# One fixed instruction sequence behind the first block, and decayed k turned by VectorE and DRAM transfers

## The chip, the core and the metric

The kernel runs on one core of one Trainium2 chip. The core has five engines that work side by side, each through its own list of instructions in order: TensorE (PE, with weight loads shown apart as PEld), VectorE (DVE), ScalarE (ACT), GpSimd (POOL) and SyncE (SP), which issues most of the transfers. They wait for each other by semaphores. The metric is the device time of the program in microseconds; the median of three runs stands for a kernel.

## The reference

Two computations follow each other. The first is a linear recurrence over 768 steps, for 4 batches and 8 heads with 48 features; the second is a gated feed-forward block on the 3072 resulting rows.

```python
f = 1.0 / (1.0 + np.exp(-f_logit))
for t in range(S):
    state = f[:, :, t, :, None] * state + np.einsum('bhd,bhe->bhde', k[:, :, t], v[:, :, t])
    y[:, :, t] = np.einsum('bhd,bhde->bhe', q[:, :, t], state)
x = np.ascontiguousarray(y.transpose(0, 2, 1, 3)).reshape(B * S, H * D)      # 3072 x 384
g = x @ w_gate                                                             # 384 x 1536
silu = g * (1.0 / (1.0 + np.exp(-g)))
return (silu * (x @ w_val) @ w_out).astype(np.float32)                     # 1536 x 384
```

All of it is float32. The weights may come as 64-bit floats, in which case the kernel turns their bits into float32 itself.

## The kernel before, in words

The function `short_path` holds all the work that is timed; `general_path` runs behind it only if a flag says that some decay was too small for it.

**Attention.** The sequence is cut into six chunks of 128 steps. A unit is one batch and one chunk, so that there are 24. Inside a unit the recurrence is done by matmuls. Of the gates, running products are made from the back (`tail`, L527) and from the front (`head`, L552); k is multiplied by the first (`kT`, L550) and q by the second (`qT`, L553). Both lie with features on the partitions, two heads of 48 in one group of 128. The scores `sc` (L563) are eight matmuls with a contraction over 48 rows; VectorE masks them (`A`, L565). The output `y` adds 12 matmuls of the decayed state laid out in diagonal blocks with q (L587) and 16 matmuls of v with A (L596), each writing 32 partitions; ACT copies it into the token tile `xT` (L599). For the next state, the decayed k is needed with steps on the partitions: TensorE turns it in four transposes (`kt`, L570), ACT copies it out of PSUM (L572), and eight matmuls with v give `dS` (L603), which VectorE adds to the decayed state (L607). Chunk 5 needs no new state. From chunk 2 on (`SQUARES`), f, k and q are loaded in squares of 32 x 32 and turned by VectorE's own transposes (L519, L539, L540); before that TensorE turns them (L513).

**Feed-forward.** A block takes the 512 tokens of one chunk over all batches. Block 0 (`mlp_plain`) is done plainly: 12 gate and 12 value products of 512 columns (L655), while the weights are still being fetched and converted (`weight_piece`: ACT makes two parts, L455 and L457, VectorE joins them in four instructions, L463 to L467), and then the down product (L679). Blocks 1 to 5 (`mlp_fifteen`) use a bilinear scheme that makes 3 x 3 by 3 x 2 blocks with 15 products: VectorE first makes sums of tokens (`xs`, L717 to L723), and for each of four column tiles TensorE makes 15 products of two matmuls with 256 columns (L825), ACT copies the PSUM banks (L830) and VectorE combines them. A scheme with seven products follows for the down part (`down_seven`: twelve matmuls each, L923 and L977). The weights that these schemes use are sums too. They are made by VectorE in place: for half of the column tiles during block 0's down product (`weight_sums(0)`), for the other half and for the down weights during block 1.

**Order.** Block c runs beside the attention of chunk c + 1. `take_turns` emits a piece of the block, then a step of the attention, in turn. The instructions of the first chunk have a fixed order (`in_order`), and within a block some of the products are chained; otherwise a scheduler in the compiler decides, by its own reckoning of times, which instruction comes next on each engine. PSUM has eight banks: in blocks 1 to 5 two for A, one for B, two for o and c, three for attention.

Of the kernel before, what the change touches and what calls it, by code (L numbers as in the profile page):

```python
# [289 lines left out]
def short_path(ctx, tc, ident, least, judge, q, k, v, f_logit, moe_w_gate, moe_w_val, moe_w_out, out):  # L290
# [32 lines left out]
    early = ctx.enter_context(ExitStack())  # L323
    first_pool = early.enter_context(tc.tile_pool(name="first", bufs=1))
# [47 lines left out]
    decayed = const.tile([128, HP, D], FP32, tag="decayed", name="decayed")  # L372

    blocks = const.tile([128, HP, 2 * D], FP32, tag="blocks", name="blocks")
    nc.gpsimd.memset(blocks, 0.0)

    vs = [(const if i < NV // 2 else first_pool).tile([128, H, W], FP32, tag=f"v{i}", name=f"v{i}")
          for i in range(NV)]
    for t in vs:
        nc.gpsimd.memset(t[:, :, D:W], 0.0)  # L380

    w_both = const.tile([128, 2, KT, DFF], FP32, tag="w_both", name="w_both")
# [50 lines left out]
    def weight_piece(dst, src):  # L433
# [4 lines left out]

        if src.dtype == FP32:
            return (lambda: nc.sync.dma_start(out=dst, in_=src)), (lambda: None), (lambda: None)  # L440
        shape = list(dst.shape)
        kept = {}

        def fetch():
            kept["w"] = wst.tile(shape[:2] + [2 * shape[2]], I32, tag="w64", name="w64", bufs=3)
            nc.sync.dma_start(out=kept["w"], in_=src)

        def halves():
            words = kept["w"].rearrange("p a (n two) -> p a n two", two=2)
            return words[:, :, :, 0], words[:, :, :, 1]  # L450

        def sizes():
            lo, hi = halves()
            up = wst.tile(shape, I32, tag="up", name="up")
            nc.scalar.activation(up, lo.bitcast(U32), AF.Copy, scale=2.0 ** -29)  # L455
            top = wst.tile(shape, I32, tag="top", name="top")
            nc.scalar.activation(top.bitcast(FP32), hi.bitcast(FP32), AF.Abs)  # L457
            kept["up"], kept["top"] = up, top

        def join():  # L460
            lo, hi = halves()
            up, top = kept["up"], kept["top"]
# [3 lines left out]
            nc.vector.scalar_tensor_tensor(top, hi, -(1 << 30), top, op0=ALU.bitwise_and, op1=ALU.bitwise_or)  # L466
            nc.vector.tensor_tensor(dst.bitcast(I32), top, up, ALU.add)  # L467

        return fetch, sizes, join
# [10 lines left out]
    NW = 256  # L480

    def add_piece(dst, src):
        for group, f in zip((fetches, sizes, joins), weight_piece(dst, src)):
            group.append(f)

    for j in range(0, DFF, NW):
        for dst, src in ((w_gate, moe_w_gate), (w_val, moe_w_val)):
            add_piece(dst[:, :, j:j + NW], in_rows(src)[:, :, per * j:per * (j + NW)])
    for i in range(NF // 2):
        both = slice(i, NF, NF // 2)  # L490
        add_piece(w_out[:, both, :], in_rows(moe_w_out)[:, both, :])
# [12 lines left out]
    def attention(u):  # L504
# [12 lines left out]
        if c >= SQUARES:  # L517
            nc.scalar.activation(squares("f"), squares("f"), AF.Sigmoid)
            nc.vector.transpose(in_turn(pairs(gate)[:, :, 1:N1]), squares("f"))  # L519
# [3 lines left out]
        yield  # L523


# [8 lines left out]

        kT = att.tile([128, HP, C], FP32, tag="kT", name="kT")
        qT = att.tile([128, HP, C], FP32, tag="qT", name="qT")
        if c >= SQUARES:
            kp, qp = kT, qT
            nc.vector.transpose(in_turn(kT), squares("k"))  # L539
            nc.vector.transpose(in_turn(qT), squares("q"))  # L540
            load_after(u)
        else:
            kp = transposed("kTp", kr)
            qp = transposed("qTp", qr)
        if c:
            nc.vector.tensor_tensor(decayed, states[b], whole.broadcast_to((128, HP, D)), ALU.mult)
            for par in range(2):
                r = rows_of(par)
                nc.scalar.copy(blocks[r, :, par * D:(par + 1) * D], decayed[r])
        nc.vector.tensor_tensor(kT, kp, pairs(tail, 2)[:, :, 0:C], ALU.mult)  # L550
        head = att.tile([128, n], FP32, tag="head", name="head", bufs=1)
        nc.vector.tensor_tensor_scan(head, gate[:, 0:n], start, 1.0, op0=ALU.mult, op1=ALU.add)  # L552
        nc.vector.tensor_tensor(qT, qp, pairs(head)[:, :, 1:N1], ALU.mult)  # L553
        if 0 < c < SQUARES:
            load_after(u)
        yield
# [3 lines left out]
        for a in range(HP):  # L560
            for par in range(2):
                r = rows_of(par)
                nc.tensor.matmul(sc[par][:, a * C:(a + 1) * C], lhsT=kT[r, a, :], rhs=qT[r, a, :], start=True, stop=True)  # L563
        for par in range(2):
            nc.vector.tensor_tensor(A[:, par], sc[par].rearrange("p (a t) -> p a t", t=C),  # L565
                                    causal.unsqueeze(1).broadcast_to((128, HP, C)), ALU.mult)
        if c < NCH - 1:
            p = bank("kt")
            for a in range(HP):
                nc.tensor.transpose(p[:, a * C:(a + 1) * C], kT[:, a, :], ident)  # L570
            kt = att.tile([128, H, W], FP32, tag="kt", name="kt")
            nc.scalar.copy(kt, p.rearrange("t (h d) -> t h d", d=W))  # L572
        yield

        if b == 0:
            xT[c] = ffn.tile([128, KT, TB], FP32, tag="xT", name="xT", bufs=2)


        y = bank("y")

        def place(n):
            return y[Q * (n % 4):Q * (n % 4) + Q, n // 4 * C:(n // 4 + 1) * C]

        per = 2 * D // Q
        if c:
            for n in range(DM // Q):
                nc.tensor.matmul(place(n), lhsT=blocks[:, n // per, n % per * Q:(n % per + 1) * Q], rhs=qT[:, n // per, :],  # L587
                                 start=n < 4, stop=False, skip_group_check=True)
        flat = v_.rearrange("t h e -> t (h e)")
        met = {n % 4 for n in range(DM // Q)} if c else set()  # L590
        for par in range(2):
            for n in range(DM // Q):
                h = 2 * (n // per) + par
                at = n * Q - h * D
                if -Q < at < D:
                    nc.tensor.matmul(place(n), lhsT=flat[:, W * h + at:W * h + at + Q], rhs=A[:, par, n // per, :],  # L596
                                     start=n % 4 not in met, stop=par == 1 or at + Q <= D, skip_group_check=True)
                    met.add(n % 4)
        nc.scalar.copy(xT[c][:, :, b * C:(b + 1) * C], y[:, 0:DM].rearrange("p (a t) -> p a t", t=C))  # L599
        if c < NCH - 1:  # L600
            p = bank("dS")
            for h in range(H):
                nc.tensor.matmul(p[W * (h % 2):W * (h % 2) + W, (h // 2) * D:(h // 2 + 1) * D],  # L603
                                 lhsT=kt[:, h, :], rhs=v_[:, h, 0:D], start=True, stop=True)
            dS = p[:, 0:HP * D].rearrange("p (a d) -> p a d", d=D)
            if c:
                nc.vector.tensor_tensor(states[b], decayed, dS, ALU.add)  # L607
            else:
                nc.scalar.copy(states[b], dS)
        yield  # L610

    def load_after(u):

        w = u + (1 if units[u][1] >= SQUARES else 2)
        if w < len(units) and (units[w][1] >= SQUARES) == (w == u + 1):
            load(w)

    def attention_steps(c):

        runs = [attention(c * B + b) for b in range(B)]  # L620
        parts = [1, 2, 1, 1]
# [27 lines left out]
    def mlp_plain(c):  # L649
        h = {}  # L650

        def product(w, j, name):
            p = fps.tile([128, 512], FP32, tag="m", name=name)[:, 0:TB]
            for i in range(KT):
                nc.tensor.matmul(p, lhsT=w[:, i, j * 128:(j + 1) * 128], rhs=xT[c][:, i, :],  # L655
# [17 lines left out]
        return ([lambda j=j, f=f: f(j) for i in range(0, NF, 2) for f in (gate, val) for j in (i, i + 1)],  # L673
# [8 lines left out]
    def put_out(p, c, b):  # L682
        ob = ffn.tile([128, 2, DM], FP32, tag=f"ob{b % 2}", name="ob", bufs=1)[:, 0, :]
# [487 lines left out]
```

## Time and the profile before

| | |
|---|---|
| median of three runs | 632.69 us (630.79, 632.69 and 632.91) |
| the profiled execution, its whole time | 630.66 us |
| its span, first to last instruction | 628.9 us |
| VectorE busy | 497.9 us (79%) |
| ScalarE busy | 297.4 us (47%) |
| transfers on SP's queue | 84,144 packets, 42.68 MB, 28.6% of 16 DMA engines' time |
| first gate product of block 0 starts | 33.22 us |
| first product of block 1 starts | 146.88 us |
| last matmul ends | about 623.8 us |

A row of the profile names the line, the engine, the operation, what it writes and reads (`sc<-qT,kT`), its tile and a count. In rows of TensorE each float32 matmul has two records, so that `x16` is eight matmuls. A matmul's duration reaches into the next one's, since they are pipelined: how fast TensorE goes is read from start to start. In the table of stretches each row gives the stretch, its length, and the busy time of PE, PEld, DVE, ACT and POOL with the number of instructions; then the clock granted to TensorE and the share of the DMA engines' time.

### The profile page before, as it was taken

To read this page: it belongs to the slowest core of one execution; us is meant where nothing else is said; L and a number is where in the kernel's file an instruction comes from. 1 tells how busy PE (TensorE), PEld (TensorE's weight loads), DVE (VectorE), ACT (ScalarE), POOL (GpSimd) and SP (SyncE) were. 2 spreads that over 40 slices of the span, in tenths; PEclk is the share of its full clock that TensorE was granted. 3 is DMA by queue.
4 is the path that set the end of the run, shared out by engine and by line. 5 is a ranking of instruction groups with operands and counts; after the bars stand their busy time and mean duration, and the time that the engine had idled before them with its cause. 6 is when DMAs were issued, how large, how long until landed. Compare 5 with 4: busy or idle time off the path is not lost.

```text
span 628.9 us, 11292 instructions
## 1 busy us (share of the span) xinstructions
PE 611.1 (97%) x4420; PEld 494.2 (79%) x4420; DVE 497.9 (79%) x941; ACT 297.4 (47%) x546; POOL 3.2 (1%) x22
## 2 busy tenths in 40 slices
PE   7899999999999999999999999999999999999996
PEld 4744555666877899888889888889988889988896
DVE  7887889968999997589897479987678994357641
ACT  2463657214667812667631556650365540166600
POOL 1000000000000000000000000000000000000000
PEclk9999999999999999999999999999999999999999
DMA  9997465024222204122213213322301200100001
GB/s 152 237 223 236 146 177 163 3 67 134 62 67 76 73 21 123 38 66 71 69 39 89 75 27 74 83 60 69 97 27 39 64 1 1 52 1 2 0 1 55
DMA packets 87517, 48.00 MB, mean 76 GB/s; under 512 B 53664, under 2 KB 81312, under 8 KB 87456
## 3 DMA queue, kind: packets, MB, share of 16 engines
q1 hardware_dynamic: 84144, 42.68, 28.6%
q10 hardware_dynamic: 3312, 4.52, 2.0%
q8 instruction: 36, 0.59, 0.4%
q14 instruction: 25, 0.20, 0.1%
HBM read 42.47 MB, written 4.72 MB: 75 GB/s over the span
## 4 chain that ended last, share of the span: by engine, by line
PE 80%; DVE 10%; DMA 4%; ACT 4%; issue 1%; SPq 0%; ACTq 0%; DVEq 0%
PE o L923 17%; PE A L825 13%; PE B L825 11%; PE o L679 5%; PE gate L655 5%; PE val L655 5%; PE o L825 4%; PE c L825 4%; PE sc L563 3%; PE o L977 3%; PE y L596 2%; PE y L587 2%; DVE c L720 2%; PE kt L570 1%; DVE h L842 1%
## 5 line engine op out<-in xcount | busy, mean ns | idle before, releaser
L923 PE MATMUL o<-w_out,h 128*128 128x192 f32 x360 | 62.5, 330 | 1.2 <-ACT c L940 0.7
L825 PE MATMUL A<-xs,w_both 128*128 128x256 f32 x240 | 62.0, 380 | 0.0
L923 PEld LDWEIGHTS o<-w_out,h 128*128 128x128 f32 x360 | 58.2, 190 | 3.0 <-ACT c L940 1.5
L717 DVE TENSOR_TENSOR c<-c,aside 128x512 f32<-128x512 f32 x60 | 41.7, 695 | 21.3 <-ACT aside L830 20.5
L830 ACT COPY c<-A 128x512 f32<-128x512 f32 x40 | 23.4, 586 | 61.7 <-PE A L825 61.6
L830 ACT COPY aside<-A 128x512 f32<-128x512 f32 x60 | 35.2, 586 | 32.3 <-PE A L825 32.2
L825 PEld LDWEIGHTS A<-xs,w_both 128*128 128x128 f32 x240 | 45.1, 190 | 6.2
L842 DVE TENSOR_TENSOR h<-h,c 128x256 f32<-128x256 f32 x100 | 41.8, 426 | 7.6 <-ACT h L841 7.6
L720 DVE TENSOR_TENSOR c<-c,aside 128x512 f32<-128x512 f32 x60 | 41.7, 696 | 2.1 <-ACT aside L830 1.8
L841 ACT ACTIVATE h<-c 128x256 f32<-128x256 f32 x100 | 41.8, 421 | 2.4 <-DVE c L717 1.2
L825 PE MATMUL A<-xs,extra 128*128 128x256 f32 x160 | 41.3, 380 | 1.6 <-ACT c L830 0.9
L825 PE MATMUL B<-xs,w_both 128*128 128x256 f32 x160 | 41.9, 384 | 0.2
L825 PE MATMUL B<-xT,extra 128*128 128x256 f32 x160 | 41.6, 382 | 0.0
L825 PE MATMUL c<-xT,w_both 128*128 128x256 f32 x160 | 41.3, 380 | 0.0
L923 PE MATMUL o<-ws,h 128*128 128x192 f32 x240 | 41.0, 327 | 0.0
L830 ACT COPY aside<-B 128x512 f32<-128x512 f32 x60 | 35.0, 584 | 9.9 <-PE B L825 9.6
L923 PEld LDWEIGHTS o<-ws,h 128*128 128x128 f32 x240 | 39.0, 190 | 0.2
L720 DVE TENSOR_TENSOR c<-o,c 128x512 f32<-128x512 f32 x40 | 28.1, 703 | 13.2 <-PE o L825 12.7
L563 PEld LDWEIGHTS sc<-qT,kT 48*128 48x128 f32 x384 | 25.7, 187 | 12.9 <-issue 9.4
L825 PEld LDWEIGHTS A<-xs,extra 128*128 128x128 f32 x160 | 30.2, 190 | 6.5 <-ACT c L830 1.3
L599 ACT COPY xT<-y 128x384 f32<-128x384 f32 x24 | 11.5, 477 | 49.8 <-PE y L596 49.8
L565 DVE TENSOR_TENSOR A<-sc,causal 128x512 f32<-128x512 f32 x48 | 31.1, 688 | 3.9 <-PE sc L563 3.9
(127 smaller groups left out, 1197.1 us busy)
## 6 DMA issues: line engine op xcount, KB each, us to landing
fsquares<-in_f_logit_dram SPq DMA_DIRECT2D x64, 96.0 KB, 2.3
ksquares<-in_k_dram SPq DMA_DIRECT2D x64, 96.0 KB, 2.3
qsquares<-in_q_dram SPq DMA_DIRECT2D x64, 96.0 KB, 2.4
v<-in_v_dram SPq DMA_DIRECT2D x24, 192.0 KB, 3.7
w<-in_moe_w_gate_dram SPq DMA_DIRECT2D x6, 768.0 KB, 6.5
w<-in_moe_w_val_dram SPq DMA_DIRECT2D x6, 768.0 KB, 5.9
w<-in_moe_w_out_dram SPq DMA_DIRECT2D x6, 768.0 KB, 4.5
out_dram<-ob ACTq DMA_DIRECT2D x23, 192.0 KB, 1.9
```

The source lines that it names most:

```text
L563: nc.tensor.matmul(sc[par][:, a * C:(a + 1) * C], lhsT=kT[r, a, :], rhs=qT[r, a, :], start=True, stop=True)
L565: nc.vector.tensor_tensor(A[:, par], sc[par].rearrange("p (a t) -> p a t", t=C), causal.unsqueeze(1).broadcast_to((128, HP, C)), ALU.mult)
L655: nc.tensor.matmul(p, lhsT=w[:, i, j * 128:(j + 1) * 128], rhs=xT[c][:, i, :], start=(i == 0), stop=(i == KT - 1))
L679: nc.tensor.matmul(p, lhsT=h[n // 2][:, n % 2 * 2 + b // 2, b % 2 * C:(b % 2 + 1) * C], rhs=w_out[:, j, :], start=(n == 0), stop=(n == NF ...
L717: nc.vector.tensor_tensor(dst, a, b, ALU.add)
L720: nc.vector.tensor_tensor(dst, a, b, ALU.subtract)
L825: nc.tensor.matmul(p[name][:, n, :], lhsT=weights_of[a][:, n, cols], rhs=tokens[b], start=fresh and n == 0, stop=True, skip_group_check=True)
L830: nc.scalar.copy(t, p[name])
L841: nc.scalar.activation(dst, src[:, 0, :], AF.Silu)
L842: nc.vector.tensor_tensor(dst, dst, src[:, 1, :], ALU.mult)
L923: nc.tensor.matmul(p[:, n, :], lhsT=lhsTs[j][:, n * C:(n + 1) * C], rhs=rhs[:, j, :], start=first and j == 0 and n == 0, stop=j == NP - 1, ...
L977: nc.tensor.matmul(p3[:, n, :], lhsT=h[j][:, 2, n * C:(n + 1) * C], rhs=b22[:, j, :], start=n == 0 and j == 0, stop=j == NP - 1, skip_grou ...
```

## The change

Behind block 0 one fixed order for TensorE, VectorE, ScalarE and SP takes the place of the scheduler's. Attention is cut into 14 steps in place of five. Each step, each token sum and each weight sum has a place on a time axis written into the code, in which a product counts 0.86 and a down product 3.9; the steps are emitted between the products when their place has come. Results of VectorE that follow a product are emitted one piece later (`lag`).

Further parts of it:

- From chunk 2 to chunk 4, decayed k isn't turned by TensorE. VectorE transposes it in squares of 32 x 32 into `beside`, four transfers write these to a tile in DRAM, in runs of 128 bytes, and a fifth reads them back as `kt`, 2 KB for each of the 128 partitions.
- For batches 0 to 2 of every chunk but the first, y is made with eight matmuls of the decayed state (48 rows, 64 columns) and eight of v (128 rows, 64 columns) in two banks. ACT copies them into `yT`, and ten transfers bring the heads to their places in `xT`. Batch 3 still uses diagonal blocks and one copy.
- The sums of both halves of the weights are made in block 0; the first weight pieces are converted in halves, and the first products are ordered gate, value, gate, value, with the transposes of the next unit between them. Weights lie in tiles of 128 columns.
- Loads of f, k and q and loads of v are issued at different steps; four outputs of block 0 are copied by ACT and VectorE in turn; in the down part the even columns come first.

The core of the diff:

```diff
+    turn_pool = ctx.enter_context(tc.tile_pool(name="turn", bufs=2, space=bass.MemoryType.DRAM))
...
-    w_both = const.tile([128, 2, KT, DFF], FP32, tag="w_both", name="w_both")
+    w_both = const.tile([128, 2, NF, KT, 128], FP32, tag="w_both", name="w_both")
...
+            nc.vector.tensor_tensor(decayed[:, :, 0:D], states[b], whole.broadcast_to((128, HP, D)), ALU.mult)
+        if c and b == B - 1:
+            diagonal = att.tile([128, HP, 2 * D], FP32, tag="x", name="diagonal")
+            nc.gpsimd.memset(diagonal, 0.0)
+            for par in range(2):
+                nc.scalar.copy(diagonal[rows_of(par), :, par * D:(par + 1) * D], decayed[rows_of(par), :, 0:D])
+        yield
+
+        kt = att.tile([128, HP * C], FP32, tag="kt", name="kt")
+        if SQUARES <= c < NCH - 1:
+            beside = att.tile([128, n], FP32, tag="head", name="beside", bufs=1)[:, 0:HP * C]
+            beside = beside.rearrange("p (i m) -> p i m", i=NI)
+            nc.vector.transpose(beside.rearrange("p i (a e) -> p a i e", e=Q), kT.rearrange("p a (i e) -> p a i e", e=Q))
+            turn = turn_pool.tile([Q, NI, HP, NI, Q], FP32, tag="turn", name="turn")
+            for r in range(NI):
+                nc.sync.dma_start(out=turn[:, :, :, r, :].rearrange("t i a e -> t (i a) e"),
+                                  in_=beside[Q * r:Q * (r + 1)].rearrange("t i (a e) -> t (i a) e", e=Q))
+            nc.sync.dma_start(out=kt, in_=turn.rearrange("t i a r e -> i t (a r e)"))
         yield
...
-        if c < NCH - 1:
-            p = bank("kt")
-            for a in range(HP):
-                nc.tensor.transpose(p[:, a * C:(a + 1) * C], kT[:, a, :], ident)
-            kt = att.tile([128, H, W], FP32, tag="kt", name="kt")
-            nc.scalar.copy(kt, p.rearrange("t (h d) -> t h d", d=W))
+        if c < SQUARES:
+            p = bank("kt")
+            for a in range(HP):
+                nc.tensor.transpose(p[:, a * C:(a + 1) * C], kT[:, a, :], ident)
+        yield
+        if c < SQUARES:
+            nc.scalar.copy(kt, p)
...
+        if c and b < B - 1:
+            y = [bank("y") for _ in range(2)]
+            def place(a, par):
+                return y[par][W * (a % 2):W * (a % 2) + W, a // 2 * C:(a // 2 + 1) * C]
+            for a in range(HP):
+                for par in range(2):
+                    r = rows_of(par)
+                    nc.tensor.matmul(place(a, par), lhsT=decayed[r, a, :], rhs=qT[r, a, :],
+                                     start=a < 2, stop=False, skip_group_check=True)
+            for par in range(2):
+                for a in range(HP):
+                    nc.tensor.matmul(place(a, par), lhsT=v_[:, 2 * a + par, :], rhs=A[:, par, a, :],
+                                     start=False, stop=a >= HP - 2, skip_group_check=True)
+            yT = att.tile([128, 2, HP // 2 * C], FP32, tag="x", name="yT")
+            for par in range(2):
+                nc.scalar.copy(yT[:, par, :], y[par][:, 0:HP // 2 * C])
...
+                    nc.sync.dma_start(out=xT[c][f % 128:f % 128 + n, f // 128, b * C:(b + 1) * C],
+                                      in_=yT[r:r + n, par, a // 2 * C:(a // 2 + 1) * C])
...
+    PRODUCT, DOWN = 0.86, 3.9
+    STEPS = (-2.6, -1.3, 0, 1.3, 2.8, 3.5)
+    UNITS_2 = [[at + t for t in STEPS] + [*rest] for at, rest in (
+        (2.6, (4, 9, 9.1, 12, 14, 17.3, 20, 21)), (12.5, (18.2, 24, 24.1, 28, 30, 34.5, 36, 37.5)),
+        (28.5, (35, 41, 41.1, 51.4, 52.5, 57, 57, 58)), (52, (57.1, 64, 64.1, 68, 70, 72.5, 76, 77.2)))]
+    UNITS = [[at + t for t in STEPS] + [*rest] for at, rest in (
+        (-10, (-6, 1, 1.1, 6, 8, 10.5, 14, 15)), (6.5, (12, 18, 18.1, 22.5, 24.5, 27, 31, 32)))] + UNITS_2[2:]
...
-    for c in range(NCH):
...
-        take_turns(pieces, attention_steps(c + 1) if c + 1 < NCH else [], 2 if c else 8)
...
+    for c in range(2, NCH):
+        for b in range(B):
+            run = attention(c * B + b)
+            waiting += [((c - 2) * whole + t, lambda run=run: next(run)) for t in (UNITS_2 if c == 2 else UNITS)[b]]
...
+    for c in range(1, NCH):
+        come_in(now)
+        for took, f in blocks[c]:
+            come_in(now)
+            before = lagging[:]
+            lagging.clear()
+            f()
+            for g in before:
+                g()
+            now += took
...
+    in_order(mark, (mybir.EngineType.PE, mybir.EngineType.DVE, mybir.EngineType.Activation, mybir.EngineType.SP))
```

The eight places behind `STEPS` in a row of `UNITS` are, in order: the transpose of q and the next unit's loads; qT and the decayed state; kt by VectorE and transfers; the scores; A; y; dS; the new state.

## The prediction, made before the changed kernel was run

> **What bounds the kernel now.** I read the page's totals first, then a table of seven stretches, then the instructions of TensorE (PE) in order of time. The stretches end where VectorE (DVE) makes the token sum `xs<-xs,xT`, once in each block of tokens (L723, at 140.90, 242.55, 341.75, 440.83 and 534.25 us), so that each holds one block's work.
>
> ```profile
> PE 611.1 (97%) x4420; PEld 494.2 (79%) x4420; DVE 497.9 (79%) x941; ACT 297.4 (47%) x546; POOL 3.2 (1%) x22
> ...
> PE 80%; DVE 10%; DMA 4%; ACT 4%; issue 1%; SPq 0%; ACTq 0%; DVEq 0%
> ```
>
> ```profile
> 0.00:33.20 33.20, 26.65 (x343) 19.52 (x344) 27.62 (x50) 12.95 (x23) 2.91 (x19) 1.00 1.15 194
> 33.20:140.90 107.70, 107.70 (x628) 58.56 (x627) 89.71 (x149) 49.97 (x70) 0.24 (x3) 1.00 0.55 144
> 140.90:242.55 101.65, 97.51 (x750) 81.78 (x749) 99.30 (x185) 55.75 (x104) 0.00 (x0) 1.00 0.29 76
> 242.55:341.75 99.20, 98.38 (x773) 85.23 (x772) 80.86 (x159) 52.81 (x98) 0.00 (x0) 1.00 0.26 68
> 341.75:440.83 99.08, 98.37 (x778) 86.06 (x778) 81.09 (x160) 50.23 (x96) 0.00 (x0) 1.00 0.25 65
> 440.83:534.25 93.42, 93.42 (x697) 82.36 (x697) 71.90 (x146) 42.03 (x86) 0.00 (x0) 1.00 0.14 37
> 534.25:628.90 94.65, 89.07 (x463) 80.71 (x461) 47.41 (x101) 33.67 (x70) 0.00 (x0) 1.00 0.05 18
> ```
>
> Behind the length stand the busy times of PE, weight loads, DVE and ACT, then the granted clock (1.00 everywhere). PE is the bound, except in the third stretch, where DVE works 99.30 of 101.65 us. A busy PE isn't a fast one, though. What it loses is seen in the order of its instructions in block 2:
>
> ```profile
> 253.61 0.49 PE L563 MATMUL sc<-qT,kT 48*128 48x128 f32 x2
> 254.03 1.13 PE L825 MATMUL B<-xT,extra 128*128 128x256 f32 x4
> ...
> 261.99 0.48 PE L563 MATMUL sc<-qT,kT 48*128 48x128 f32 x2
> 262.41 1.13 PE L825 MATMUL B<-xT,extra 128*128 128x256 f32 x4
> ...
> 286.22 1.16 PE L563 MATMUL sc<-qT,kT 48*128 48x128 f32 x16
> 287.31 0.66 PE L570 MATMUL kt<-idf,kT 128*128 128x128 f32 x4
> 287.80 1.03 PE L825 MATMUL o<-xs,extra 128*128 128x256 f32 x4
> ```
>
> From start to start, a product of L825 takes 0.865 us, a whole score group 1.09, four kt transposes 0.49. In the same way y takes 1.69 (12 matmuls of L587 and 16 of L596), dS 0.60. Going into or out of a narrow tile costs 0.10 each (286.22 is 0.96 behind the product before it, not 0.865). A single score matmul that the scheduler put alone (253.61, 261.99) costs 0.52 with its two switches, where it would take 0.14 inside a group.
>
> So a block with attention beside it needs 60 products x 0.865 + 7 x 3.90 (twelve down matmuls) + 4 units x 4.17 (scores and kt 1.68, y and dS 2.49, switches included) = 95.9 us. It takes 99.2. Of the 3.3 about 2.3 are split groups (one unit's scores in three pieces, another's y and scores in two) and 1 us waits.
>
> **The change, part by part.**
>
> *Whole groups in a fixed order.* In the new instruction order sc, y and dS of each unit stand in one piece on PE. The split cost goes (-2.3 in blocks 2 and 3). DVE results come one product later than now, but their PSUM banks are used again three products (2.6 us) later, and ACT, at half load, copies them. What is late next: at the end of the products two table loads (1.28 each), a sigmoid and four Silus stand on ACT before the last down matmuls, about 4 us against 3.2 us of scores and first down half; I leave 0.8 us of wait in each block.
>
> *kt by VectorE and DRAM (blocks 2 to 4, 12 units).* PE loses 4 transposes, -0.49; but scores then return to a wide tile without the transposes between, +0.10, and dS now stands apart from y, +0.20. Net -0.19 a unit, -0.8 a block. ACT loses one copy of 0.585. DVE gains one 32x32 transpose at the 1.14 us of the kT row L539 (0.96 from start to start): +4.0 a block, beside PE, covered where DVE has 18 us free (blocks 2, 3). Without that cover (block 1) it is paid in full.
>
> Here a rule speaks against the change. The Trainium skill, "VectorE: DVE Perf Modes", Rules for kernel authors, gives 128x128 transposes to TensorE when PSUM will do, and its section on the three transpose paths warns that VectorE turns only 32x32 blocks and that a DMA with rearranged strides is slow. By the rule the 12 units are the wrong way round: 0.49 of PE against 1.14 of DVE and five DMAs. By the rows PE is the full engine, and DVE and DMA (26% busy) aren't, so I take the rows: -0.8 a block instead of a loss.
>
> *The round trip.* SP issues four writes (the squares loads give 1.74 for four), then waits for them and issues one read. Landing isn't shown for SBUF to DRAM in runs of 128 B; between 2.3 (squares) and 3.7 (v, whose runs are 192 B). With the DVE transpose it is 1.14 + 1.74 + 2.3..3.7 + 0.44 + 2.3..3.7 = 7.9 to 10.7 us. The timetable puts kt 10.9 to 15.9 us before dS, and sc and y between them add about 3. I take it as hidden. Behind the read on SP stand the output pieces and the next unit's loads; these have some 6 us of their own. `beside` uses the buffer of `head`, so the next unit's scan waits for the four writes (5.2 to 6.6 by the same terms), 6.9 us after in the tightest unit: just hidden; without it DVE would stand.
>
> *y of units 0 to 2.* 8 matmuls of 48x64 and 8 of 128x64 take the place of 28. Not in the trace. Bounds: if the first eight run four abreast as L587 does (0.23 a four) and the others two abreast as a score pair does (0.23 to 0.27), 1.5 with 0.1 for the switch between the two shapes; if the first run only two abreast, 2.1. The Trainium skill, "TensorEngine Tiling (Array Packing)", Key Properties, says that a change of mode drains the array; the trace's 0.10 is that. I take 1.6, nearest the 64x64 case: -0.1 each, -1.5 over 15 units, range -3 to +6. Two ACT copies replace one (+0.3, free), and ten small DMAs on SP carry y to xT (4.4 us of issue); tokens need them only at the block's end.
>
> *Weight sums to block 0.* About 10 of the odd-half sums (0.60 each) and some DVE idle time move ahead. Counting DVE's new order at the trace's paces: block 0 goes from 79 to 92 us in 105; block 1 from 99.2 to 95.2; blocks 2 and 3 from 78.6 to 82.6. So block 1 stays DVE's, at 95.2 plus some 2.3 of waits that a fixed order can't fill: 97.5.
>
> *The opening.* The first gate product now starts at 33.22, behind three transposes that wait for q (landed by 32.8). In the new order it follows dS of the last unit (over at 30.4), and its weights come in halves: VectorE's four joins take 1.5 instead of 3. Up to -2.5; but VectorE delivers the last hidden weights at 96.2, used at 101.1, and has more to do: I take -1.8 (0 to -2.5). The four copies out of the last down banks are split over ACT and DVE: the 1.4 us wait `o L825 <- ACT ob L684` shrinks by about 1.0.
>
> **Sum**, against the profiled execution (630.66, span 628.9): opening -1.8, block 0 -0.3, bank -1.0, block 1 101.65 to 97.5 -4.1, block 2 99.2 to 95.6 -3.6, block 3 -3.5, block 4 (no kt, no dS; only split groups go) 93.4 to 92.0 -1.4, end -0.4: -16.1, so **614.5**. The profiled execution lies 2.0 below the median of 632.69, but inside the three runs' 630.79 to 632.91; I keep 614.5.
>
> **Rivals.**
> *The timetable fits exactly* (0.17): no waits stay, opening kept at -2.5, y at its lower bound. Block 1 at PE's 94.8, blocks 2 and 3 at 94, block 4 at 91, -1.5 in block 0 and bank: about -24, **607**. For it: the constants 0.86 and 3.9 in the code are the trace's own. Against: block 1's DVE sum.
> *VectorE becomes the bound* (0.13): in a fixed queue each wait on ACT or a DMA is lost. Blocks 1 to 3 gain only half, the opening nothing: -16.1 + 5.6 + 1.8 = -8.7, **622**. For it: the 20 us windows between 280 and 300 already show DVE at 19.72.
> *The round trip is late* (0.10, slower): SP is one in-order queue with loads, 30 output pieces and 20 kt transfers a block. If it takes 17 us against 14.5 of cover, PE, whose order is fixed, stands 2.5 us at each of 12 dS: +30 - 16 = +14, **645**. It turns the sign at 15.8 us, and the estimate is 8 to 11.
> *No gain* (0.04): the waits move from PE's split groups to its bank waits; -2 to +2, **631**.
> The forecast has 0.56.
>
> **From cases to numbers.** What a measurement can tell from no change is 0.5%, 3.2 us. Faster: 0.56 + 0.17 + 0.13 = 0.86; same 0.04; slower 0.10. The forecast's own range is 608 to 621; with the rivals 604 to 627 leaves out the late round trip, no gain and the edges.
>
> **What would show it.** No kt transposes behind 145 us and 16 whole score groups; `dS` on PE without a wait on the kt transfer; stretches near 97.5, 95.6, 95.6 and 92; DVE near 95 in block 1; first gate product near 31. Wrong if PE waits for kt, if y takes over 2 us, or if weights arrive late in block 0.

## The result, and the profile after

The changed kernel takes **622.91 us** (median of four runs, 621.62 to 623.55) against 631.96 for the kernel before, run beside it: a ratio of 0.9855, 95% interval 0.9829 to 0.9881. The profiled execution took 623.06 us, with a span of 621.3 (before: 630.66 and 628.9). The interval is clear of 1, so it is faster. It lies 8.4 us above the forecast of 614.5: outside the forecast's own range of 608 to 621, inside the wide one of 604 to 627. By the medians the gain is 9.1 us, by the profiled executions 7.6 of the 16.1 that were forecast.

Three lines of the page of the changed kernel: the engines' busy times, the granted clock in 40 slices of the span (15.5 us each), and the chain that ended last by engine.

```profile
PE 599.1 (96%) x4012; PEld 484.5 (78%) x4012; DVE 507.1 (82%) x973; ACT 287.5 (46%) x523; POOL 5.0 (1%) x27
...
PEclk9998999999999999999999999999999999999998
...
PE 67%; DVE 12%; DMA 8%; SPq 4%; ACT 4%; issue 3%; ACTq 0%; DVEq 0%
```

TensorE works 12.0 us less, yet the span is only 7.6 shorter: idle time has come in. In the chain, DMA went from 4% to 8% and SP's queue from 0 to 4%. And the clock has an 8 in slice 4, where the kernel before shows 9 throughout. (The 8 in the last slice, and the 0.97 in the last row below, lie behind the last matmul, at 614.10, and cost nothing.)

The token sums, at which the prediction cut its stretches, were moved by the change. So the stretches below begin at the first product of each block instead: the opening, block 0, blocks 1 to 4, block 5 with the end (columns as in the table before).

```profile
0.00:31.33 31.33, 23.99 (x331) 17.77 (x332) 25.82 (x48) 10.47 (x20) 2.64 (x19) 1.00 1.21 196
31.33:149.17 117.84, 115.91 (x584) 63.82 (x585) 104.39 (x185) 55.41 (x78) 0.67 (x4) 0.99 0.52 142
149.17:247.36 98.19, 96.32 (x689) 82.76 (x688) 92.35 (x173) 49.58 (x92) 0.42 (x1) 1.00 0.41 101
247.36:343.77 96.41, 95.25 (x690) 83.26 (x689) 82.35 (x163) 46.72 (x89) 0.42 (x1) 1.00 0.38 94
343.77:440.62 96.85, 95.25 (x690) 83.26 (x689) 83.23 (x165) 46.71 (x89) 0.42 (x1) 1.00 0.39 95
440.62:533.45 92.83, 92.34 (x627) 81.22 (x626) 71.84 (x142) 44.84 (x87) 0.42 (x1) 1.00 0.20 52
533.45:621.30 87.85, 80.06 (x410) 72.41 (x409) 47.08 (x102) 33.79 (x70) 0.00 (x0) 0.97 0.05 15
```

Set beside the kernel before, whose blocks start at 33.22, 146.88, 250.07, 350.19, 449.26 and 542.99 (where one product of a block, or half of one, stood ahead of the last down matmuls, it is counted back at 0.86 a product; the prediction cut its stretches elsewhere, so that differences are compared and not lengths):

| | before | after | difference | predicted |
|---|---|---|---|---|
| opening | 33.22 | 31.33 | -1.9 | -1.8 |
| block 0 | 113.66 | 117.84 | **+4.2** | -0.3 |
| block 1 | 103.19 | 98.19 | -5.0 | -5.1, with the bank |
| block 2 | 100.12 | 96.41 | -3.7 | -3.6 |
| block 3 | 99.07 | 96.85 | -2.2 | -3.5 |
| block 4 | 93.73 | 92.83 | -0.9 | -1.4 |
| block 5 to the last matmul | 80.78 | 80.66 | -0.1 | } -0.4 |
| last matmul to the end | 5.13 | 7.22 | **+2.1** | } |
| span | 628.9 | 621.3 | -7.6 | -16.1 |

The loss sits at both ends, and a little in block 3. For block 0, these are TensorE's rows from 48 us on:

```profile
48.17 1.88 PE L731 MATMUL val<-xT,w_both 128*128 128x512 f32 x4
51.85 1.16 PE L601 MATMUL sc<-qT,kT 48*128 48x128 f32 x16 [1.81 <-DVE qT L569]
52.95 1.12 PE L605 MATMUL kt<-idf,kT 128*128 128x128 f32 x4
53.86 4.85 PE L731 MATMUL val<-xT,w_both 128*128 128x512 f32 x8
```

TensorE stands 1.81 us for qT, which VectorE makes between joins of weights (it is busy 9.60 of the 10 us from 50 to 60). Then comes something the sum did not have: four kt transposes take 0.91 instead of 0.49, and four value matmuls (eight records) 4.7 instead of 3.4. The clock granted in the stretches of 2 us around it, next to last but one in each row, says why:

```profile
51.00:53.00 2.00, 1.15 (x17) 1.05 (x17) 2.00 (x6) 0.00 (x0) 0.00 (x0) 0.99 1.04 392
53.00:55.00 2.00, 2.00 (x7) 1.48 (x7) 2.00 (x4) 1.14 (x2) 0.00 (x0) 0.50 1.09 260
55.00:57.00 2.00, 2.00 (x4) 0.75 (x4) 1.64 (x4) 1.05 (x2) 0.00 (x0) 0.66 0.88 305
57.00:59.00 2.00, 2.00 (x6) 0.80 (x6) 2.00 (x4) 0.15 (x1) 0.00 (x0) 1.00 0.34 53
```

For block 3, SP's transfers and the two ends of the turn, in order of time:

```profile
413.54 6.55 SPq L643 DMA_DIRECT2D xT<-yT  x10
420.19 0.53 SPq L431 DMA_DIRECT2D v<-in_v_dram  x1
420.82 1.95 SPq L427 DMA_DIRECT2D fsquares<-in_f_logit_dram  x4
422.80 0.71 DVE L588 STREAM_TRANSPOSE beside<-kT 128x512 f32<-128x512 f32 x1
422.86 1.80 SPq L427 DMA_DIRECT2D ksquares<-in_k_dram  x4
424.76 1.80 SPq L427 DMA_DIRECT2D qsquares<-in_q_dram  x4
426.66 3.62 SPq L591 DMA_DIRECT2D turn<-beside  x4
431.85 0.58 SPq L593 DMA_DIRECT2D kt<-turn  x1
...
437.97 0.67 PE L673 MATMUL dS<-v,kt 128*64 128x48 f32 x16 [1.12 <-DMA kt<-turn]
```

`beside` is done at 423.5; its writes are issued 3.2 us later, behind what is left of the next unit's twelve loads. These start late themselves, since the ten token transfers of the unit before hold the queue from 413.54 to 420.1. The read is issued at 431.85 and dS can start 6.1 later. From the transpose to dS that is 15.2 us.

### The profile page after: what moved, and what is told of

Read it like the earlier page. It is cut to its first block, busy times and chain, and to the rows that moved or that the text cites. A ratio compares the mean times of both kernels' runs of the same rounds, so it can differ in the third digit from the quotient of the medians.

```text
span 621.3 us, 10926 instructions
## 1 busy us (share of the span) xinstructions
PE 599.1 (96%) x4012; PEld 484.5 (78%) x4012; DVE 507.1 (82%) x973; ACT 287.5 (46%) x523; POOL 5.0 (1%) x27
## 4 chain that ended last, share of the span: by engine, by line
PE 67%; DVE 12%; DMA 8%; SPq 4%; ACT 4%; issue 3%; ACTq 0%; DVEq 0%
PE o L1009 13%; PE A L906 12%; PE B L906 10%; PE o L756 5%; PE o L906 4%; PE val L731 4%; DMA kt<-turn 4%; PE c L906 3%; PE gate L731 3%; PE sc L601 3%; SPq L427 2%; PE y L632 2%; PE o L1073 2%; DVE c L808 2%; PE dS L673 1%
## 5 line engine op out<-in xcount | busy, mean ns | idle before, releaser
L922 ACT ACTIVATE h<-c 128x256 f32<-128x256 f32 x100 | 39.2, 416 | 2.0 <-DVE c L808 0.9
L906 PEld LDWEIGHTS B<-xs,w_both 128*128 128x128 f32 x160 | 30.3, 190 | 4.8 <-ACT c L911 0.7
L906 PEld LDWEIGHTS c<-xT,w_both 128*128 128x128 f32 x160 | 30.2, 190 | 4.7 <-DVE c L808 0.3
```

Source lines behind the costliest of these rows:

```text
L906: nc.tensor.matmul(p[name][:, n, :], lhsT=weights_of[a][:, n, j, :], rhs=tokens[b], start=fresh and n == 0, stop=True, skip_group_check=True)
L922: nc.scalar.activation(dst, src[:, 0, :], AF.Silu)
```

## The experiments

All are the changed kernel with the edit named. "Block 2" and so on are lengths as in the table above, from one profiled execution; the whole time is the median of all.

**Decayed k by TensorE again.**

```diff
-        if SQUARES <= c < NCH - 1:      # beside, turn, kt
+        if False:
-        if c < SQUARES:                 # four transposes behind the scores, ACT's copy
+        if c < NCH - 1:
```

> The changed kernel, but decayed k is turned by TensorE in chunks 2 to 4 too (four transposes behind the scores, ACT copies); everything else stays. Theory A (the turn through DRAM saves PE little and partly gives it back): TensorE pays 0.39 for each of 12 units (+4.7 us), the waits of dS for kt (2.6 us) go, and block 1, where VectorE is busy 94.6 of 98.2 us, is relieved of four transposes of 0.71: about -2 there. Sum near zero, -1 to +1 against 622.9. Rival B (the turn is hidden and its whole price is saved): +4.7, 627.6, block 1 not shorter. Rival C (the transfers disturb the loads of the units): more than 2 us faster than 622.9.

622.3 us, ratio 0.9853 (0.9838 to 0.9867): the changed kernel's own. Block 1 97.41, blocks 2 and 3 97.00 and 97.01 (up 0.6 and 0.2), no wait of dS. Block 1 is 0.8 shorter, not the 2 expected (VectorE was busy 92.35 us in it, as the row above has it, and not 94.6). Theory A: the turn gives nothing on balance.

**y with diagonal blocks again, and then with their copy moved.**

```diff
-        if c and b == B - 1:            # diagonal tile, filled by ACT at qT's place
+        if c:
-        if c and b < B - 1:             # new y and its ten transfers
+        if False:
```

> The changed kernel, but y of all batches is made with diagonal blocks and one copy into the token tile, as before the change; no small transfers from yT. Theory A (the new y saves what the trace shows, 1.52 against 1.69 with its switches): +0.17 to +0.22 for each of 15 units, +2.5 to +3.3, less up to 1 us because SP has 150 transfers less ahead of kt: 624 to 626. Rival B (the SP queue is what delays kt of the fourth unit, and it is worth more than the matmuls): dS no longer waits (2.6 us), and the kernel is not slower than 622.9.

633.6 us, ratio 1.0045 (1.0032 to 1.0058), 11 us worse: neither theory. dS no longer waits, but TensorE waits 13.5 us for PSUM banks (7.5, 4.8 and 1.2, for c and aside). One such wait, VectorE's, ACT's and TensorE's rows:

```profile
205.09 0.35 DVE L573 TENSOR_TENSOR decayed<-state,tails 128x192 f32<-128x192 f32 x1
...
205.53 0.71 ACT L579 COPY diagonal<-decayed 48x192 f32<-48x192 f32 x2 [2.50 <-DVE decayed L573]
...
206.26 0.42 ACT L922 ACTIVATE h<-c 128x256 f32<-128x256 f32 x1
...
206.59 0.57 ACT L911 COPY c<-A 128x512 f32<-128x512 f32 x1
...
207.21 1.13 PE L906 MATMUL A<-xs,extra 128*128 128x256 f32 x4 [1.35 <-ACT c L911]
```

ACT's queue is fixed. It stands 2.50 us for `decayed` with a bank full behind it, and TensorE stands in turn. To tell the form of y from the place of its copy, the next kernel moves the copy only:

```diff
-            for par in range(2):        # at qT's place
-                nc.scalar.copy(diagonal[rows_of(par), :, par * D:(par + 1) * D], decayed[rows_of(par), :, 0:D])
         A = att.tile([128, 2, HP, C], FP32, tag="A", name="A")
+        if c:
+            for par in range(2):
+                nc.scalar.copy(diagonal[rows_of(par), :, par * D:(par + 1) * D], decayed[rows_of(par), :, 0:D])
```

> As the run with diagonal y (y of all batches by diagonal blocks), but ACT copies the decayed state into the diagonal tile at the place of the scores, not at that of qT. Theory A (in that run 11 us were lost because ACT stood behind VectorE's decayed state while PSUM banks waited to be copied; the matmuls themselves cost 0.26 for each of 15 units, 3.9): the waits of TensorE for c and aside fall from 13.5 to under 4 us; since dS doesn't wait for kt, whole time 622.5 to 626. Rival B (the diagonal form itself costs 0.8 for each unit): stays near 633.

622.13 us, ratio 0.9843 (0.9826 to 0.9859). The bank waits are 2.1 us, dS waits 0.4, blocks 1 to 4 take 98.19, 96.26, 96.25 and 93.25. In block 4, which has no kt, the new y is 0.42 shorter for three units, and in block 2 without its wait (96.41 - 0.68) 0.53: 0.14 to 0.18 each, some 2.3 us over 15 units. Its 150 transfers give that back ahead of kt on SP, as the same place in block 3 shows:

```profile
414.69 0.39 SPq L431 DMA_DIRECT2D v<-in_v_dram  x1
...
420.74 1.74 SPq L427 DMA_DIRECT2D qsquares<-in_q_dram  x4
424.41 3.83 SPq L589 DMA_DIRECT2D turn<-beside  x4
429.82 0.56 SPq L591 DMA_DIRECT2D kt<-turn  x1
```

Without the token transfers v and the loads are issued from 414.69 on instead of 420.19, and are through when `beside` is done, at 424.38. The writes go out at once, the read 2 us earlier than in the changed kernel although `beside` is 0.9 later, and dS doesn't wait.

**Block 0's attention two pieces later.**

```diff
-            want = min(i + 1, n) * len(second) // n
+            want = max(min(i + 1 - 2, n), 0) * len(second) // n
```

> The changed kernel, but in block 0 each attention step comes two pieces later, so that the first scores stand behind two more products. Theory A (the stop of 1.95 us ahead of the first scores brings on the fall of the granted clock that follows): stop and fall both go, the stretch 50 to 60 us shows a clock of 1.00 instead of 0.83, and the first product of block 1 starts 3.6 us earlier, near 145.6; whole time near 619.3. Rival B (the clock falls for another reason): only the stop goes, -1.9, clock still under 0.9 for some 10 us. Rival C (VectorE is the bound of block 0): TensorE stands somewhere else in block 0 for as long, no gain.

623.17 us, ratio 0.9872 (0.9858 to 0.9886). The stop ahead of the first scores is gone and the clock from 50 to 60 is 1.00, but a wait of 1.54 for VectorE's last `h` has appeared ahead of the down matmuls, at 107.96. Block 0 takes 115.91, 1.9 less, but in this execution dS waits 5.3 us for kt in blocks 1 to 3, instead of 2.6. Four executions of other kernels here that kept the stop and still had the full clock took 116.17 to 116.63. So rival C holds for the stop: it moves. Theory A holds at most for the clock, of which more below.

**The turn on another queue.**

```diff
-                nc.sync.dma_start(out=turn[...], in_=beside[...])
-            nc.sync.dma_start(out=kt, in_=...)
+                nc.gpsimd.dma_start(out=turn[...], in_=beside[...])
+            nc.gpsimd.dma_start(out=kt, in_=...)
```

> The changed kernel, but the five transfers of the turn of decayed k are issued by GpSimd instead of SyncE, so that they no longer stand behind the twelve loads and ten token transfers on SyncE's queue. Theory A (the place in the queue makes kt late): dS no longer waits for kt (2.6 to 5.7 us in all, in the runs so far), blocks 1 to 3 fall to near 97.5, 95.8 and 95.7, whole time 3 to 5 us less. Rival B (the transfers themselves are slow beside the loads): the wait of dS stays over 2 us. Rival C (GpSimd's issue is dear or disturbs VectorE): kt later than now, slower.

622.3 us, ratio 0.9853 (0.9833 to 0.9873). Block 2 falls to 95.86 almost without a wait, as A has it, but block 3 takes 99.68, with a wait of 2.02 instead of 1.12 and a fall of the clock to 0.50 behind it:

```profile
424.13 2.54 POOL L591 DMA_DIRECT2D turn<-beside  x4 [2.48 <-DVE beside L588]
...
431.46 0.70 POOL L593 DMA_DIRECT2D kt<-turn  x1 [4.79 <-DMA turn<-beside]
...
438.57 0.67 PE L673 MATMUL dS<-v,kt 128*64 128x48 f32 x16 [2.02 <-DMA kt<-turn]
```

The writes are issued 2.5 us earlier than in the changed kernel, but read and wait end no earlier: the read starts 4.79 after the last write is issued and takes another 7. So in block 3 it is the transfers beside the loads that are slow (B), in block 2 the queue (A). The loads are there at that time because the token transfers still hold them back on SP (they are issued from 420.45 on): with y in diagonal blocks, above, neither wait is left, on the one queue.

**No fixed order behind block 0** (the last `in_order` taken out).

> The changed kernel without the fixed order behind block 0: the program is emitted by the same time axis, but the compiler's scheduler decides the order. Theory A (the fixed order is what gains 2.3 us a block by whole groups, and lowers the waits in blocks 1 to 3): blocks 1 to 4 each 1 to 3 us longer than 98.5, 96.7, 97.0 and 92.8, scores split again; whole time 627 to 633. Rival B (the emitted order is the gain, whoever keeps it): within 1 us of the changed kernel.

645.69 us, ratio 1.0225 (1.0192 to 1.0258), slower than the kernel before. Blocks 1 to 3 take 99.88, 97.04 and 98.56, block 4 114.41. SP's and TensorE's rows at its start, then the clock:

```profile
433.15 11.64 SPq L643 DMA_DIRECT2D xT<-yT  x4
444.89 0.59 SPq L593 DMA_DIRECT2D kt<-turn  x1
```

```profile
450.19 1.10 PE L673 MATMUL dS<-v,kt 128*64 128x48 f32 x16 [5.36 <-DMA kt<-turn]
451.22 2.08 PE L601 MATMUL sc<-qT,kT 48*128 48x128 f32 x16
```

```profile
450.00:460.00 10.00, 9.19 (x95) 7.66 (x96) 4.96 (x13) 1.18 (x3) 0.42 (x1) 0.50 0.70 151
```

The scheduler put token pieces, which wait for yT, ahead of the read of kt on SP; dS stands 5.36 us, and then TensorE works at half clock (scores 2.08 instead of 1.09) until 460.98, and again for 6.83 us from 498.53 on. By an estimate, the stop and half of the 10.8 and 6.8 us worked at half clock make 14 of the 21.6 us by which block 4 is longer. So a late round trip is dear, and the changed kernel's order for SP, with the read ahead of those pieces, avoids this one; no run frees SP's order alone. "Scores split again" missed: 15 of the 16 score groups from block 1 on stay whole, and 7 of the 12 new y groups are cut in two. Whole score groups come with the order in which the program is emitted, then, whoever keeps it. What whole groups are worth, the next two runs ask:

**Both new forms undone, and then score groups split.** The first joins the edit of k with the second edit of y. The second adds this:

```diff
                 nc.tensor.matmul(sc[par][...], lhsT=kT[r, a, :], rhs=qT[r, a, :], start=True, stop=True)
+                if a == 0 and c >= SQUARES:
+                    yield                # a product of the block comes between
```

> The changed kernel with both new forms undone: decayed k is turned by TensorE everywhere, and y of all batches is made with diagonal blocks, their copy at the place of the scores. The fixed order, the opening and the place of the weight sums stay. Theory A (the two new forms give TensorE some 5 us, and their transfers take them back in waits and falls of the clock): within 1.5 us of the changed kernel, 621.5 to 624; no wait of dS; blocks 2 and 3 near 97.4. Rival B (they are worth what they save on TensorE, 0.39 for each of 12 units and 0.15 for each of 15): 6 to 7 us slower, near 629.

> As the run with both new forms undone, but the score group of each unit from chunk 2 on is cut into three pieces (1, 1 and 6 matmuls, in the fourth unit 2 and 6), with a product of the block between. Theory A (a score matmul that stands alone costs 0.52 instead of 0.14 inside its group): +0.38 for each of six pieces a block and about 0.3 for the fourth unit, +2.6 a block in blocks 1 to 4, +10 in all. Rival B (a switch costs nothing that other work doesn't hide): within 1.5 us of the unsplit one.

Without either form: 622.53 us, ratio 0.9862 (0.9847 to 0.9877), blocks 1 to 4 97.55, 97.40, 97.42 and 93.25. Split: 637.62, ratio 1.0106 (1.009 to 1.0121), 15.1 more where theory A had 10. Blocks 2 and 3 take 100.60 each, 3.2 more, block 4 2.9 more. Block 1 takes 5.9 more, because its first scores, which the edit also moves forward, wait 1.81 us for qT, and the clock falls behind that stop. TensorE's rows of one split unit in block 2:

```profile
254.68 1.03 PE L913 MATMUL B<-xT,extra 128*128 128x256 f32 x4
255.63 0.48 PE L602 MATMUL sc<-qT,kT 48*128 48x128 f32 x2
256.05 1.13 PE L913 MATMUL o<-xs,extra 128*128 128x256 f32 x4
257.11 0.48 PE L602 MATMUL sc<-qT,kT 48*128 48x128 f32 x2
```

From 255.63 to 257.11 a lone score matmul and a product take 1.48; less the product's 0.865 that is 0.62, against 0.14 inside the group. It was priced at 0.52. Per block seven more pieces cost 3.2, or 0.46 each. So the timetable with its fixed order and what came with it (whole groups, the opening, the place of the weight sums) make all of the measured gain, and the two new forms, as they stand together, none.

**The last stores.** First only the seventh down product's sums were taken out of `lag`, and its halves laid in two banks; then the fifth's as well:

```diff
+        soon = (lambda f, *args: f(*args)) if c == NCH - 1 else lag
...
-                lag(plus, kept["u"], kept["u"], kept["p"])
+                soon(plus, kept["u"], kept["u"], kept["p"])
...
-            if n == 0:
+            if n == 0 or c == NCH - 1:
                 kept["p"] = bank2("o3", "A")
...
-            lag(plus, kept["o", 0][:, n, DH:DM], kept["u5"][:, n, :], kept["p"][:, n, :])
+            soon(plus, kept["o", 0][:, n, DH:DM], kept["u5"][:, n, :], kept["p"][:, n, :])
```

> The changed kernel, but in the last block the two halves of the last down product lie in two banks, and the sum and the store of the first half follow it at once instead of one piece later. Theory A (the first half's sum waits for all 24 matmuls, so two stores land together at the end): from the last matmul to the end 7.2 us falls to 5.1 as before the change, whole time -2.0, near 620.9. Rival B (the three stores on ACT's queue land late whatever starts them): under -0.7.

> The changed kernel, but in the last block the sums and stores of the fifth and the seventh down product follow at once, in VectorE's order too, and the two halves of the seventh lie in two banks. In the earlier try the first half's sum had come ahead of the fifth product's sums on VectorE, so that these went out 1.7 us later. Theory A (two stores that land together make the tail): the first store of the first half is issued 2 us before the last matmul ends, from the last matmul to the end 6.2 to 7.2 falls to 5.1; whole time -1.3 to -2. Rival B (the tail is the transfer's own): stays over 6.2.

The first missed: 624.78 us, ratio 0.9903 (0.9887 to 0.9918), end 7.0 us. The first half's sum, no longer lagged, stood ahead of the fifth product's lagged sums in VectorE's queue, and the first of those stores left as the last matmul ended, instead of 2.2 us ahead of it. The second: 625.08 us, ratio 0.9886 (0.9862 to 0.991), end 5.58. VectorE's and the queues' rows of the changed kernel, then of the second edit:

```profile
610.83 1.02 DVE L805 TENSOR_TENSOR ob<-c,o 128x384 f32<-128x384 f32 x2
611.88 3.04 ACTq L1018 DMA_DIRECT2D out_dram<-ob  x3
614.14 0.62 DVE L805 TENSOR_TENSOR ob<-c,o 128x192 f32<-128x192 f32 x2 [2.29 <-PE o L1073]
614.83 0.38 SPq L1018 DMA_DIRECT2D out_dram<-ob  x1
```

```profile
617.27 1.99 ACTq L1018 DMA_DIRECT2D out_dram<-ob  x3
617.58 0.35 DVE L805 TENSOR_TENSOR ob<-c,o 128x192 f32<-128x192 f32 x1 [0.34 <-PE o L1075]
619.53 0.35 DVE L805 TENSOR_TENSOR ob<-c,o 128x192 f32<-128x192 f32 x1 [1.59 <-PE o L1075]
619.95 0.38 SPq L1018 DMA_DIRECT2D out_dram<-ob  x1
```

Lagged, both halves' sums wait for all 24 matmuls (`x2` at 614.14), and two stores leave together. At once, the first half goes 2 us earlier. The end took 6.1 to 7.4, 6.8 on average, in ten executions without the second edit, and 5.6, 6.2 and 6.2 in the three with it (two follow below): some 0.8 of the 2.1 is explained. The rest lies in the landing of the very last store, SP's. It is issued 0.46 us behind the last matmul in the kernel before and 0.72 in the changed one, and lands 2.3 us after its issue in the one, 4.4 in the other; in the three with the edit it is issued at 0.46 and still takes 3.1, 4.2 and 3.9. Why it lands later than before the change isn't shown. The whole times of these two runs aren't better, since waits for kt came to 5.7 and 6.0 us there. Up to block 4 both run the changed kernel's own instructions, in whose profile the same wait is 2.6: it varies by as much as these edits are worth.

**Put together.** Diagonal y copied at the scores, stores at once, block 0's attention later; then also kt by TensorE in chunk 2 alone (`SQUARES < c < NCH - 1` for the turn, `c <= SQUARES` for the transposes).

> The changed kernel with three edits together: y of all batches with diagonal blocks copied at the place of the scores, the stores of the last block at once, and the attention of block 0 two pieces later. The turn of decayed k through DRAM stays. Theory A (each takes away a wait that the others leave): dS waits under 1 us, blocks 2 and 3 near 96.2, tail near 5.6, block 0 near 116: 618.5 to 620.5, faster than the changed kernel by 0.4% or more. Rival B (a wait taken away comes back at the next engine): 621.5 or more.

> As the run with three edits (diagonal y copied at the scores, the last stores at once, block 0's attention two pieces later), but chunk 2's decayed k is turned by TensorE; the turn through DRAM stays for chunks 3 and 4. Theory A (in block 1 VectorE has no room for its four transposes, so there the turn costs what it saves TensorE and more; in blocks 2 and 3 it saves 1.1 each): block 1 from 98.4 to 97.6, blocks 2 and 3 stay near 96.3, whole time 0.6 to 1.0 us less, near 619.8. Rival B (block 1 is bound by TensorE as well): block 1 goes up by 1.1 like the others without the turn, 99.5, near 621.7.

620.58 us, ratio 0.9831 (0.9818 to 0.9844), just above the range given to A: the end took 6.2. Then **619.87** us, ratio 0.9813 (0.9794 to 0.9832), the runs from 619.26 to 620.07: the fastest kernel here. All are under the changed kernel's 621.62 to 623.55, though these were taken at another time; the intervals of the two ratios just touch. Block 1 goes from 98.36 to 97.62, blocks 2 and 3 stay at 96.26 and 96.27. Against the 97.4 without the turn these are 1.14 shorter, 0.29 a unit, while in block 1 the turn costs 0.7, although TensorE has four transposes less for each unit there. VectorE, busy 92.98 of those 98.36 us with the turn and 90.76 of 97.62 without, is the likely reason; the edit takes the five transfers away too, so that this isn't shown apart.

## Why the prediction was right or wrong

**Bound and whole groups: right.** TensorE's order was where the time lay. The split cost was put at 2.3 in block 2 and in block 3. With both forms undone, they fell from 100.12 and 99.07 to 97.4, by 2.7 and 1.7. In the trace of the kernel before, block 2 has five pieces more than whole groups would make and block 3 only three; at the 0.46 of the split run that is 2.3 and 1.4. So the mechanism holds, and in block 3 its size was copied from block 2. A lone score was misread on the way: the prediction's own rows, 0.42 from start to start and two switches of 0.10, give 0.62 and not 0.52.

**Blocks 1 and 2: right, 98.19 and 96.41 against 97.5 and 95.6.** Without the waits for kt (0.78 and 0.68 us) they are at 97.4 and 95.7. In block 2 some luck is in it: the two forms gave more than was taken (1.1 and 0.5 us), and a wait that stood at nothing took 0.7 back. That block 1 stays VectorE's is borne out in part, by the last edit: without the turn it is shorter there and longer elsewhere. The 0.8 us a block left for a wait on ACT ahead of the down matmuls came to 0.2.

**"I take it as hidden": wrong.** The round trip was put at 7.9 to 10.7 against some 14.5 of cover; in block 3 it took 15.2. Three terms were too small: the place behind the loads on SP (3.2, not in the sum), the issue of the writes (3.62 against 1.74; their landing, 2.2 in the median, was within what was taken), and the read (6.1 from its issue to dS, against 2.7 to 4.1 for issue and landing). The loads beside it are the smaller part of this last: in the trace of the changed kernel the packets of a read are over 4.4 to 4.9 us after its issue where no load runs beside it, and 5.2 to 5.4 in the fourth units, where loads do. The two rows used were of other transfers, squares of 96 KB and v of 192, for a read of 256. The 3.2 goes back to the token transfers, which were counted as 4.4 us of free issue: they hold the loads back, and these then stand ahead of the writes. The waits came to 2.6 us in the profile shown and up to 6.0 in others.

**kt and y: the size of each about right, the sum of the two wrong.** Freed of waits they give 0.29 and 0.15 a unit (taken: 0.19 and 0.1), some 4 us where they fit. But the five transfers of the one and the ten of the other share one queue, and their cost was put at nothing. The run without both is as fast as the one with both. Block 3 shows all of it: 1.7 for whole groups, 1.1 for kt and 0.5 for y, less a wait of 1.1, make its 2.2 in place of 3.5.

**The rule weighed against the rows.** The Trainium skill, "VectorE: DVE Perf Modes", Rules for kernel authors, would leave these transposes to TensorE. By the rows I took the other side. In blocks 2 and 3, with SP's queue unburdened, the rows won (1.14 a block); in block 1 the rule did, and with the ten transfers beside it whole time showed no difference.

**The opening and block 0, -2.1 taken, +2.3 measured: wrong.** The first gate product does start 1.9 earlier, as priced. But the three transposes that stood ahead of it weren't removed, only moved: they now stand behind it, 3 x 0.44 = 1.3. And "VectorE has more to do" was stated and then not priced: over the block it is busy 104.39 of 117.84 us, which looks like room, but around the first scores it is busy 9.60 of 10, and TensorE stands 1.8 at the first scores, or 1.5 at the down product when they come later. That makes 3.1 of 4.2. The fall of the clock is worth some 1.6 more (117.8 to 118.3 with it, 116.2 to 116.6 without), and y and dS, at 0.6 less than before, gave some of it back.

**The end, -0.4 taken, +2.1 measured: wrong.** The lag was priced as one product of delay on banks. For the last sums it moves the first half's store from 2.2 us before the end of the last matmul to 0.5 behind it, where it leaves together with the last store. Taking the lag out there gave back 0.8 of the 2.1. The rest is in the landing of the last store, and its cause stays open.

**Rivals.** VectorE as the bound was put at 622, which is the time, but not by its steps: blocks 1 and 2 gained in full. The late round trip was put at 645, with a wait of 2.5 at each of 12 dS. The run without the fixed order took 645.7, but the number is a coincidence: only two dS waited there, 1.0 and 5.4 us, and falls of the clock did more.

## What to carry to other kernels

In a fixed order each engine's queue is part of the plan: an instruction that waits (ACT for VectorE's `decayed`, SP for yT, VectorE's lagged sums) holds up all that stands behind it, and two copies in the wrong place cost 11 us where their form costs 2. Price every transfer of a round trip from rows of its own size and direction, and count what stands before it in its queue, and what that in turn has waited for. A step moved off the start is still paid, where it lands.

## What the runs showed of the hardware

A stop of TensorE of under 2 us can cost the clock. Ten executions had the same stop of 1.81 us ahead of the first scores in block 0. In six the granted clock was 0.83 from 50 to 60 us; seen finely, in the changed kernel it was at 0.50 from 52.95, a microsecond after work had begun again, to 56.37. In the other four it stayed at 1.00, and so it did in all three kernels without the stop. The Trainium skill, "TensorE: Matmul & The Clock Gate", "Why this matters for your kernels", asks for no gaps over about 3 us; 1.8 was enough here in six cases of ten.

Where falls begin isn't free. In each execution that has several, their starts in the trace's record of the clock lie a whole number of steps of 3.4133 us apart: 52.83 and 441.95 (114 steps), 53.48 and 439.18 (113), 447.33 and 498.53 (15), and, in the changed kernel, 52.95 and 616.15, behind the last matmul (165). They last one, two or four such steps (3.41, 6.83, 13.65 us) where work goes on. So the clock is set on a grid that runs on whatever the kernel does, and that lies differently in each execution. Counted back from the fall at the end of each of the ten, the six with a fall have the stop, to within 0.05 us, inside one step, with 0.9 to 1.7 us of scores and kt transposes behind it. In the other four a point of the grid cuts the stop (51.28, 51.38) or comes under 0.3 us behind it (51.69, 51.86). That sorts all ten, but it was read off afterwards; no run moved the stop on the grid.

How much of a step must be idle stays open. Later stops of 1.81, 1.84, 2.02 and 2.62 us had such falls as well, and one of 1.25 with 1.7 us of narrow scores and y behind it; several of 1.69 to 2.26 hadn't. In the stop of 5.36 us the clock went to 0.50 after 2.5 us and stayed there 13.65 us, on through the narrow matmuls of dS, scores and y.

A 32x32 transpose of 128x512 on VectorE took 0.71 us for `beside<-kT`, but 1.1 for the squares: the two differ in the order in which they read and write, so that this order counts, and the estimate of 1.14 was too high.
